# A new order of the pieces, and new engines for 250 of them, from the last weight decodes to the end of a fused attention and cosine feed-forward kernel

## The chip, the core and the metric

The kernel runs on one core of a Trainium2 chip. The metric is the device time of one execution in microseconds (us), and the median of several executions is compared. TensorE (PE) does the matrix products, VectorE (DVE), ScalarE (ACT) and GpSimd (POOL) the work on elements, and SyncE (SP) issues nearly all DMAs.

## What is computed

Attention inside chunks of 64 tokens, then a feed-forward layer whose activation is h·cos(h):

```python
scores = scale * np.matmul(q_c, k_c.transpose(0, 1, 2, 4, 3))
scores = scores - np.max(scores, axis=-1, keepdims=True)
attn = np.exp(scores)
attn = attn / (np.sum(attn, axis=-1, keepdims=True) + 1e-09)
out = np.matmul(attn, v_c)
...
h = x @ w_in
g = h * np.cos(h)
return (g @ w_out).astype(np.float32)
```

There are 8 batches, 8 heads, 576 tokens and 64 columns a head, so x has 4608 rows of 512; w_in is 512x2048 and w_out 2048x512, both given as float64. Every large product is made of three in a rounded format (high by high, high by low, low by high), so each operand has a high part, which is a rounded copy, and a low part, which is the value less its high part.

## The kernel before

Tokens are worked in nine tiles of 512 (t = 0 to 8). Tiles 0 and 1 go through the layer directly, while the 32 weight blocks are decoded from float64 and split. From tile 2 on, block products by a scheme with seven instead of eight products (combinations of weight blocks, kept in device memory and streamed back) take the place of plain ones: `two_pairs` for tile 2, and `block_pair` with `block_products` for the tiles in twos (3 and 4, 5 and 6, 7 and 8, numbered u = 1, 2, 3). The attention of a later tile is woven into the products of an earlier one: `scores_now(t, g)` and `weighted_now(t, g)` for each half g of the heads. Each of these hands PE two pieces, one for each pair of heads, and each piece is 32 small 64x64 products.

All work is put down first as 3646 pieces by `piece(...)` (engine, length, function, the pieces that it waits for). Two tuples then decide everything else: `RANK` gives each piece its place in one list, and `ELSEWHERE` names the pieces that run on their other engine (DVE work on POOL, or ACT copies on DVE). `in_order` (L311) sorts, and a loop at L2527 issues the pieces in that order. Every engine, and SP with its DMAs, therefore executes its own pieces strictly in the order of the ranks, and a piece that waits holds up all that stand behind it on its engine. The ranks are written out by hand into the file; nothing is planned when the program is built.

Names that the steps below use, with what they run on:

- `out_piece` (L1504), `block_piece` (L1831), `prod` in `block_pair` (L1857): products on PE; line L352 in the profile. A `block_piece` of one pair is three 256-column products, `prod` is six of 512 columns.
- `prod` comes in the order A11, S3, S2, A12, S1, A22, S4. S2 waits for `copy_b` on ACT (L1018), which waits for A11; S4 waits for `add_b` on DVE, which waits for S1; with a later tile's attention to weave in, the next A11 waits for `copy_last` on ACT, which waits for S4.
- `parts_of_g` (L1535): the high part on ACT or DVE, then the low part on DVE or POOL (L369 and L367 are the copies, L373 the two-input operations).
- `sum_piece` (L1968), `w_load` (L2059), `wide_x` (L2370): sums of blocks and splits, on DVE or POOL and on ACT or DVE.
- `turned` (L612, operations at L686): six transposes on DVE, ahead of `weighted_now`; its two results are taken out of PSUM by ACT or DVE (L2365), and only then may PE use these banks for the next product.
- `g_load` (L2094): a stored sum is loaded back by SP, split by ACT or DVE and then DVE or POOL, and multiplied on PE.

```python
place = sorted(range(len(work)), key=lambda i: (rank[i], i)) if rank else range(len(work))
return [(i, work[i][8][0] if i in elsewhere else work[i][0]) for i in place]
...
for i, by in in_order(work, RANK, ELSEWHERE):
    work[i][2](*([by] if work[i][8] else []))
```

Of the kernel before, what the change touches and what calls it, by code (L numbers as in the profile page):

```python
# [95 lines left out]
    214, 240, 245, 251, 262, 258, 265, 268, 277, 266, 250, 267, 281, 284, 283, 274, 286, 290, 294, 287, 280, 291,  # L96
    306, 311, 300, 293, 314, 324, 327, 321, 313, 329, 333, 338, 331, 328, 339, 343, 344, 340, 342, 361, 362, 365,
    350, 354, 359, 371, 374, 377, 368, 379, 383, 386, 391, 375, 394, 398, 400, 401, 388, 403, 415, 419, 405, 397,
    408, 410, 418, 431, 427, 435, 439, 441, 434, 417, 438, 440, 443, 446, 444, 454, 458, 461, 452, 455, 467, 469,
    475, 0, 12, 1, 3, 4, 5, 2, 7, 8, 10, 6, 13, 19, 21, 9, 17, 23, 27, 16, 26, 31, 11, 14, 20, 24, 29, 32, 37, 41,  # L100
# [6 lines left out]
    249, 213, 239, 229, 233, 225, 248, 254, 264, 269, 278, 282, 263, 272, 243, 252, 273, 270, 271, 275, 285, 288,  # L107
    298, 302, 279, 255, 259, 276, 261, 296, 299, 304, 307, 317, 319, 301, 289, 295, 292, 297, 308, 527, 303, 305,
    309, 532, 310, 529, 548, 316, 318, 320, 322, 334, 336, 315, 330, 312, 335, 326, 325, 341, 345, 348, 351, 356,
    337, 346, 349, 332, 323, 347, 353, 357, 360, 363, 378, 358, 370, 367, 355, 352, 366, 369, 373, 376, 385, 390,  # L110
    372, 404, 409, 364, 393, 381, 387, 389, 392, 413, 416, 384, 420, 402, 380, 406, 395, 399, 407, 412, 425, 429,
    396, 428, 432, 414, 421, 453, 457, 473, 460, 464, 476, 480, 483, 487, 491, 510, 513, 545, 559, 530, 547, 555,
    556, 557, 562, 565, 572, 577, 575, 597, 576, 579, 587, 594, 598, 604, 614, 620, 636, 640, 411, 433, 430, 426,
    436, 422, 424, 442, 445, 448, 451, 437, 465, 423, 470, 447, 450, 462, 466, 471, 478, 485, 474, 449, 456, 459,
    463, 482, 484, 486, 496, 500, 504, 481, 488, 498, 468, 472, 489, 494, 502, 507, 509, 516, 505, 501, 503, 495,
    492, 512, 515, 517, 518, 523, 526, 514, 546, 511, 519, 560, 520, 528, 531, 542, 564, 567, 525, 544, 549, 535,
    522, 536, 540, 543, 550, 554, 561, 552, 537, 574, 558, 541, 569, 585, 588, 592, 595, 599, 563, 596, 584, 581,
    590, 571, 582, 591, 603, 605, 613, 602, 570, 593, 578, 586, 608, 611, 622, 625, 630, 633, 616, 628, 610, 607,
    612, 634, 638, 621, 623, 617, 629, 619, 626, 627, 631, 635, 637, 641, 642, 632, 660, 624, 643, 654, 645, 652,
    656, 667, 673, 675, 647, 676, 657, 646, 674, 659, 661, 664, 678, 691, 696, 679, 687, 665, 670, 662, 686, 689,  # L120
    697, 701, 706, 713, 704, 700, 692, 698, 720, 712, 715, 716, 719, 730, 735, 711, 737, 731, 734, 723, 721, 729,
    733, 739, 744, 748, 725, 382, 497, 534, 553, 589, 490, 658, 521, 477, 479, 493, 499, 538, 506, 508, 524, 533,
    580, 539, 551, 566, 568, 600, 573, 583, 601, 606, 609, 615, 618, 639, 644, 668, 648, 651, 672, 684, 690, 693,
    702, 650, 714, 741, 699, 709, 717, 749, 649, 655, 671, 680, 688, 722, 694, 742, 677, 732, 666, 683, 682, 710,
    669, 681, 653, 663, 724, 728, 718, 726, 736, 738, 727, 753, 756, 767, 773, 800, 802, 791, 794, 822, 824, 813,
    818, 830, 872, 885, 928, 910, 902, 916, 931, 943, 980, 992, 1007, 1031, 1008, 1020, 1075, 1049, 1072, 1079,
    1091, 1087, 1095, 1103, 1114, 1122, 1120, 1152, 1159, 1197, 1179, 1201, 1215, 1211, 752, 740, 842, 755, 766,
    759, 743, 826, 762, 785, 809, 777, 787, 880, 821, 889, 893, 817, 864, 895, 685, 695, 708, 746, 757, 764, 705,
    707, 745, 751, 775, 788, 781, 793, 796, 808, 868, 871, 878, 747, 750, 754, 758, 761, 772, 760, 763, 765, 770,
    779, 814, 806, 886, 891, 894, 904, 927, 938, 703, 768, 769, 771, 778, 776, 774, 780, 784, 783, 782, 786, 803,  # L130
    790, 789, 792, 798, 795, 799, 804, 807, 805, 812, 811, 816, 797, 801, 810, 827, 832, 836, 841, 844, 815, 820,
    825, 829, 819, 823, 828, 833, 835, 838, 862, 845, 847, 858, 851, 853, 940, 876, 896, 874, 861, 865, 921, 945,
    899, 905, 870, 883, 930, 988, 948, 890, 866, 898, 831, 834, 839, 857, 907, 909, 854, 877, 879, 884, 914, 929,
    936, 962, 964, 968, 971, 976, 979, 837, 840, 843, 846, 849, 860, 848, 852, 855, 863, 901, 961, 944, 983, 999,
    1003, 1013, 1033, 1038, 850, 856, 859, 873, 867, 869, 875, 903, 881, 882, 888, 900, 887, 892, 906, 908, 911,
    915, 913, 919, 923, 918, 922, 924, 926, 934, 897, 912, 917, 925, 952, 957, 969, 974, 920, 950, 954, 967, 932,
    935, 939, 946, 949, 953, 1036, 990, 986, 993, 981, 1024, 1040, 1048, 1055, 1074, 985, 989, 1000, 1078, 1025,
    996, 991, 1006, 1012, 1016, 1086, 1043, 933, 937, 941, 942, 951, 955, 958, 960, 959, 987, 956, 963, 977, 966,
    965, 970, 973, 998, 972, 975, 984, 995, 978, 982, 1022, 1002, 1005, 1026, 1009, 1014, 1017, 1011, 1021, 1019,
    1023, 1052, 994, 997, 1004, 1010, 1037, 1047, 1051, 1062, 1015, 1018, 1029, 1050, 1027, 1030, 1034, 1041, 1054,  # L140
    1068, 1076, 1112, 1090, 1110, 1085, 1089, 1099, 1153, 1127, 1146, 1092, 1101, 1148, 1115, 1133, 1131, 1100,
    1116, 1160, 1156, 1150, 1164, 1028, 1032, 1042, 1044, 1046, 1053, 1056, 1057, 1058, 1060, 1065, 1064, 1063,
    1067, 1071, 1073, 1070, 1080, 1083, 1082, 1081, 1094, 1118, 1097, 1102, 1161, 1105, 1108, 1163, 1107, 1111,
    1119, 1123, 1128, 1098, 1104, 1109, 1113, 1125, 1132, 1135, 1140, 1121, 1126, 1138, 1147, 1129, 1142, 1145,
    1151, 1117, 1130, 1136, 1154, 1143, 1139, 1155, 1158, 1220, 1172, 1225, 1249, 1261, 1169, 1245, 1252, 1157,
    1162, 1236, 1229, 1178, 1176, 1167, 1168, 1231, 1250, 1181, 1244, 1248, 1234, 1256, 1258, 1059, 1066, 1061,
    1084, 947, 1039, 1069, 1077, 1141, 1174, 1173, 1185, 1088, 1134, 1144, 1149, 1182, 1192, 1170, 1093, 1177, 1186,
    1001, 1045, 1096, 1137, 1180, 1184, 1124, 1165, 1190, 1195, 1175, 1189, 1106, 1199, 1035, 1191, 1166, 1171,
# [2434 lines left out]
```

## Time and profile before

| what | us |
|---|---|
| median of 3 executions | 771.12 |
| lowest and highest of them | 770.82, 772.03 |
| the profiled execution | 769.23 |
| its span, first to last instruction | 767.4 |
| PE busy in the span | 753.0 |
| DVE, ACT, POOL busy | 678.1, 530.0, 345.0 |

The page of the profile gives shares of the whole span. The timeline gives instructions in order of time with the idle time of their engine before them; the windows give busy time by stretch. A busy PE is not always a PE at its full rate, since the ends of products are modelled: what counts is the distance from one start to the next, 216 ns for a product of 512 columns here.

### The profile page before, as it was taken

The numbers are of one execution on the slowest core, as the hardware profiler recorded it, in microseconds if no ns is written. First come the engines' busy times: TensorE is split into PE (matmuls) and PEld (weight loads), VectorE is DVE, ScalarE is ACT, GpSimd is POOL, SyncE is SP. The second block draws the span as 40 slices with busy tenths as digits, with TensorE's granted clock in tenths as the row PEclk, the third lists the DMA queues.
The fourth block names the chain that finished last, engine by engine and source line by source line (L and its number), as shares of the span: only waits on it lengthen the run. The fifth ranks groups of instructions, "written<-read, shape, count | busy, mean of one in ns | idle before, by whom it ended". The sixth has DMA issues, their size and how long they took to land.

```text
span 767.4 us, 18052 instructions
## 1 busy us (share of the span) xinstructions
PE 753.0 (98%) x6676; PEld 681.3 (89%) x6676; DVE 678.1 (88%) x1138; ACT 530.0 (69%) x1066; POOL 345.0 (45%) x329
## 2 busy tenths in 40 slices
PE   7999999999999999999999999999999999999998
PEld 6888888888999888888889997888899989989997
DVE  6998889888999998989999979989999889878975
ACT  6999786466875557878786659779786566567532
POOL 3421244635599316746622246547501136464233
PEclk9999999999999999999999999999999999999999
DMA  9994332199988948888899946899899567999982
GB/s 340 410 420 156 131 125 95 58 308 361 343 298 298 315 152 294 293 307 259 310 345 378 368 166 227 284 307 325 286 383 341 170 199 250 306 314 335 362 286 91
DMA packets 127000, 210.92 MB, mean 275 GB/s; under 512 B 11712, under 2 KB 67008, under 8 KB 126912
## 3 DMA queue, kind: packets, MB, share of 16 engines
q1 hardware_dynamic: 126336, 208.71, 78.4%
q8 instruction: 53, 0.87, 0.4%
q10 hardware_dynamic: 576, 1.05, 0.4%
q14 instruction: 35, 0.29, 0.1%
HBM read 148.90 MB, written 60.82 MB: 273 GB/s over the span
## 4 chain that ended last, share of the span: by engine, by line
PE 73%; DVE 8%; DMA 7%; ACT 5%; issue 3%; POOL 2%; SPq 1%; ACTq 0%; POOLq 0%; DVEq 0%
PE acc L352 31%; PE h L352 26%; PE a L352 16%; DMA sums<-w_in 4%; DVE w_in L373 2%; DVE w_in L1027 1%; ACT w_in L1024 1%; POOL w_in L373 1%; DMA sums<-g 1%; ACT w_in L1031 1%; SPq L349 1%; DVE w_in L686 1%; DVE w_in L1021 1%; DMA w_in<-diffs 1%; DMA kt<-in_kT_dram 1%
## 5 line engine op out<-in xcount | busy, mean ns | idle before, releaser
L352 PE MATMUL h<-x,w_in 128*128 128x512 f32 (+1 forms) x960 | 224.8, 365 | 0.4 <-DVE w_in L373 0.2
L352 PEld LDWEIGHTS h<-x,w_in 128*128 128x128 f32 x960 | 169.0, 190 | 22.1 <-DVE w_in L373 0.7
L352 PE MATMUL acc<-w_out,g_hi 128*128 128x512 f32 (+1 forms) x720 | 172.7, 330 | 0.0
L352 PEld LDWEIGHTS acc<-w_out,g_hi 128*128 128x128 f32 x720 | 123.8, 190 | 12.4
L352 PE MATMUL acc<-w_out,g_lo 128*128 128x512 f32 (+1 forms) x360 | 117.4, 326 | 0.0
L352 PE MATMUL h<-w_in,w_in 128*128 128x512 f32 (+1 forms) x384 | 98.6, 355 | 1.2 <-ACT h L1018 1.1
L373 POOL TENSOR_TENSOR w_in<-w_in,w_in 128x512 f32<-128x512 f32 (+2 forms) x41 | 48.9, 1197 | 60.2 <-ACT w_in L1031 24.5
L352 PEld LDWEIGHTS h<-w_in,w_in 128*128 128x128 f32 x384 | 65.4, 190 | 10.9 <-ACT h L1018 2.9
L352 PEld LDWEIGHTS acc<-w_out,g_lo 128*128 128x128 f32 x360 | 68.6, 190 | 4.7
L369 ACT CAST g_hi<-w_in 128x512 fp32r<-128x512 f32 x71 | 44.0, 623 | 33.4 <-PE acc L352 9.2
L1031 ACT ACTIVATE w_in<-w_in 128x512 f32<-128x512 f32 x96 | 57.7, 627 | 12.1 <-DVE w_in L1027 11.8
L373 POOL TENSOR_TENSOR g_lo<-w_in,g_hi 128x512 fp32r<-128x512 f32 x32 | 42.1, 1315 | 36.5 <-ACT g_hi L369 17.9
L373 DVE TENSOR_TENSOR g_lo<-w_in,g_hi 128x512 fp32r<-128x512 f32 x62 | 45.5, 738 | 4.2 <-ACT g_hi L369 3.5
L369 ACT CAST g_hi<-x 128x512 fp32r<-128x512 f32 x52 | 32.2, 624 | 21.8 <-PE acc L352 12.3
L1024 ACT ACTIVATE w_in<-w_in 128x512 int32<-128x512 f32 x56 | 34.2, 627 | 16.8 <-DVE w_in L1021 11.9
L373 POOL TENSOR_TENSOR g_lo<-x,g_hi 128x512 fp32r<-128x512 f32 x9 | 12.2, 1362 | 74.2 <-ACT g_hi L369 74.2
L373 POOL TENSOR_TENSOR g_lo<-g,g_hi 128x512 fp32r<-128x512 f32 x18 | 23.6, 1314 | 45.9 <-ACT g_hi L369 19.9
L352 PE MATMUL a<-w_in,w_in 128*128 128x512 f32 (+1 forms) x204 | 43.1, 350 | 1.0 <-ACT w_in L369 0.7
L352 PE MATMUL a<-x,w_in 128*128 128x512 f32 (+1 forms) x192 | 41.2, 353 | 0.0
L352 PE MATMUL acc<-w_in,g_hi 128*128 128x256 f32 x240 | 41.0, 275 | 0.0
L1027 DVE SCALAR_TENSOR_TENSOR w_in<-w_in,w_in 128x512 f32<-128x512 int32 x56 | 37.8, 698 | 3.4 <-ACT w_in L1024 2.8
L373 DVE TENSOR_TENSOR g_lo<-x,g_hi 128x512 fp32r<-128x512 f32 x47 | 36.5, 789 | 4.5 <-ACT g_hi L369 4.2
(317 smaller groups left out, 1953.0 us busy)
## 6 DMA issues: line engine op xcount, KB each, us to landing
w_in<-combo SPq DMA_DIRECT2D x84, 512.0 KB, 5.5
w_in<-sums SPq DMA_DIRECT2D x64, 256.0 KB, 5.0
combo<-w_in SPq DMA_DIRECT2D x56, 256.0 KB, 3.8
w_in<-combo SPq DMA_DIRECT2D x56, 256.0 KB, 5.4
x<-sums SPq DMA_DIRECT2D x48, 256.0 KB, 5.0
qt<-in_qT_dram SPq DMA_DIRECT2D x36, 256.0 KB, 5.2
w_in<-in_w_in_dram SPq DMA_DIRECT2D x16, 512.0 KB, 9.3
kt<-in_kT_dram SPq DMA_DIRECT2D x32, 256.0 KB, 5.3
```

What stands on the lines that cost most here:

```text
L349: kept(nc.sync.dma_start(out=out, in_=in_))
L352: kept(nc.tensor.matmul(*args, **kw))
L369: kept(nc.scalar.copy(out=out, in_=in_))
L373: kept(eng.tensor_tensor(out, a, b, op=op))
L686: kept(nc.vector.transpose(out=dst[o : o + BL, :, qb], in_=src[i : i + BL, :, 1 - qb]))
L1021: kept(nc.vector.tensor_tensor(out, a, b, op=ALU.add))
L1024: kept(nc.scalar.activation(g.bitcast(I32), h, AF.Identity, bias=0.25, scale=0.5 / math.pi))
L1027: kept(nc.vector.scalar_tensor_tensor(g, g.bitcast(I32), -2.0 * math.pi, h, op0=ALU.mult, op1=ALU.add))
L1031: kept(nc.scalar.activation(g, g, AF.Sin, bias=0.5 * math.pi))
```

## The change

Only the numbers in `RANK` and `ELSEWHERE` change. The pieces, their functions and what each waits for stay as they are. The ranks agree up to place 271 of 3646, about 55 us into the profiled execution; of the 962 PE pieces the first 77 keep their places.

```diff
-    214, 240, 245, 251, 262, 258, 265, 268, 277, 266, 250, 267, 281, 284, 283, 274, 286, 290, 294, 287, 280, 291,
-    306, 311, 300, 293, 314, 324, 327, 321, 313, 329, 333, 338, 331, 328, 339, 343, 344, 340, 342, 361, 362, 365,
+    214, 240, 245, 251, 262, 258, 265, 268, 276, 266, 250, 267, 280, 283, 282, 273, 285, 289, 293, 286, 279, 290,
+    304, 310, 299, 292, 314, 325, 328, 322, 312, 330, 335, 340, 332, 329, 342, 347, 349, 343, 346, 367, 370, 373,
...
 ELSEWHERE = (
     4, 8, 9, 13, 18, 19, 23, 24, 29, 33, 34, 38, 39, 48, 53, 54, 58, 59, 63, 69, 78, 83, 98, 103, 108, 113, 114,
-    119, 123, 124, 128, 129, 134, 138, 143, 154, 158, 182, 184, 186, 188, 211, 270, 271, 287, 299, 321, 331, 355,
+    119, 123, 129, 133, 134, 138, 139, 154, 159, 182, 184, 186, 188, 211, 270, 271, 287, 299, 321, 331, 355, 365,
...
```

Read out of the two pairs of tuples, by sorting the pieces by their ranks, one engine at a time:

| attention pieces on PE | places on PE before | places after |
|---|---|---|
| scores, tile 3, g 0 | 172, 175 | 170, 171 |
| weighted, tile 3, g 0 and g 1 | 243, 244; 248, 249 | 246 to 249 |
| weighted, tile 4, g 0 and g 1 | 273, 274; 278, 280 | 275 to 278 |
| weighted, tile 5, g 0 | 367, 373 | 371, 372 |
| scores, tile 6, g 0 | 396, 398 | 398, 399 |
| weighted, tile 6, g 0 | 435, 437 | 435, 436 |
| weighted, tile 7, g 1 | 601, 603 | 605, 606 |

Runs of attention pieces on PE with no other product in them: 38 before, 30 after.

| engine changes | to | count |
|---|---|---|
| ACT copies | DVE | 59 |
| DVE copies | ACT | 41 |
| DVE two-input pieces | POOL | 75 |
| POOL two-input pieces | DVE | 75 |

Pieces on DVE: 1084 before, 1102 after; on ACT 837 and 819; on POOL 275 and 275; on SP 488 and 488. Of the net 18 copies that DVE takes over, 16 copy 512 columns inside SBUF and 2 take a result out of PSUM. Between the 163rd PE piece (172.8 us in the profiled execution) and the 446th (388.2 us) stand 304 DVE pieces before and 317 after.

## Rows read from the trace of the kernel before

**Rows 1.** Page: busy us (share of the span) by engine; the chain that ended last
```profile
PE 753.0 (98%) x6676; PEld 681.3 (89%) x6676; DVE 678.1 (88%) x1138; ACT 530.0 (69%) x1066; POOL 345.0 (45%) x329
PE 73%; DVE 8%; DMA 7%; ACT 5%; issue 3%; POOL 2%; SPq 1%; ACTq 0%; POOLq 0%; DVEq 0%
```
**Rows 2.** Timeline, PE, around attention runs: start, length, operands, count, idle before
```profile
210.78 0.38 PE L352 MATMUL acc<-w_out,g_lo 128*128 128x512 f32 x1
...
213.18 0.70 PE L352 MATMUL acc<-w_out,g_hi 128*128 128x512 f32 x2
...
250.16 0.60 PE L352 MATMUL acc<-w_out,g_hi 128*128 128x512 f32 x2
250.60 0.38 PE L352 MATMUL acc<-w_out,g_lo 128*128 128x512 f32 x1
...
252.00 0.92 PE L352 MATMUL acc<-w_out,w_in 128*128 128x512 f32 x3
...
253.83 0.38 PE L352 MATMUL acc<-w_out,g_lo 128*128 128x512 f32 x1
...
254.76 0.70 PE L352 MATMUL acc<-w_out,g_hi 128*128 128x512 f32 x2
```
**Rows 3.** Windows: us, busy time (instructions) by engine, PE clock, DMA share, GB/s
```profile
172.00:380.00 208.00, 207.67 (x2048) 184.10 (x2047) 190.64 (x317) 148.55 (x350) 124.96 (x126) 1.00 0.87 295
222.00:276.00 54.00, 54.00 (x586) 49.25 (x586) 50.04 (x79) 32.93 (x63) 34.83 (x35) 1.00 0.87 294
350.00:400.00 50.00, 48.15 (x464) 42.61 (x457) 47.47 (x82) 42.67 (x97) 27.93 (x28) 1.00 0.89 303
763.80:767.40 3.60, 0.00 (x0) 0.00 (x0) 0.42 (x1) 0.00 (x0) 0.00 (x0) 0.81 0.34 114
```
**Rows 4.** Timeline, PE, at its longest stops behind 300 us
```profile
381.64 1.56 PE L352 MATMUL a<-w_in,w_in 128*128 128x512 f32 x6 [0.70 <-ACT w_in L369]
395.06 0.49 PE L352 MATMUL a<-w_in,g_hi 128*128 128x256 f32 x2 [0.74 <-ACT g_hi L369]
395.86 0.38 PE L352 MATMUL a<-w_in,g_lo 128*128 128x256 f32 x1 [0.31 <-DVE g_lo L373]
466.08 0.48 PE L352 MATMUL h<-w_in,w_in 128*128 128x512 f32 x1 [0.27 <-ACT h L1018]
558.34 0.49 PE L352 MATMUL a<-w_in,g_hi 128*128 128x256 f32 x2 [1.35 <-ACT w_in L369]
627.45 0.48 PE L352 MATMUL h<-w_in,w_in 128*128 128x512 f32 x1 [0.34 <-ACT h L1018]
```
**Rows 5.** Timeline, PE, at a small stop ahead of the product S4
```profile
372.88 1.46 PE L352 MATMUL a<-x,w_in 128*128 128x512 f32 x6
374.43 0.92 PE L352 MATMUL h<-w_in,w_in 128*128 128x512 f32 x3
```
**Rows 6.** Timeline, SP and ACT, ahead of the stop at 558 us
```profile
551.10 2.74 SPq L349 DMA_DIRECT2D x<-sums  x4
557.20 0.61 ACT L369 CAST g_hi<-x 128x512 fp32r<-128x512 f32 x1
```
**Rows 7.** Groups by line: busy us, mean ns of one; then two rows of DVE's timeline
```profile
L369 ACT CAST g_hi<-w_in 128x512 fp32r<-128x512 f32 x71 | 44.0, 623 | 33.4 <-PE acc L352 9.2
L367 DVE CAST w_in<-w 128x512 fp32r<-128x512 f32 x11 | 4.6, 419 | 0.1
L373 POOL TENSOR_TENSOR g_lo<-w_in,g_hi 128x512 fp32r<-128x512 f32 x32 | 42.1, 1315 | 36.5 <-ACT g_hi L369 17.9
L373 DVE TENSOR_TENSOR g_lo<-w_in,g_hi 128x512 fp32r<-128x512 f32 x62 | 45.5, 738 | 4.2 <-ACT g_hi L369 3.5
753.77 1.53 DVE L373 TENSOR_TENSOR g_lo<-w_in,g_hi 128x512 fp32r<-128x512 f32 x1
758.01 1.28 DVE L373 TENSOR_TENSOR x<-g,x 128x512 fp32r<-128x512 f32 x2
```
**Rows 8.** Timeline, ACT, ahead of the stop at 381.64 us
```profile
381.00 0.59 ACT L369 COPY w_in<-a 128x512 f32<-128x512 f32 x1 [0.66 <-DVE w_in L686]
```

399 rows, old and new, of tables (ELSEWHERE, RANK) are left out of this document.

## The prediction

> **What bounds the kernel now.** I read the page first: PE is busy for 753.0 of 767.4 us, and the chain that ended last is PE for 73% [rows 1]. DVE is next with 678.1 us. So the order of the work can win only what PE loses between its products. The windows come second: of the 14.4 us in which PE is idle by the page, 3.6 lie behind the last product [rows 3], and some more in the opening, which the change leaves alone. Third, the timeline of PE alone, since a busy PE hides two kinds of loss. One is the change between 128x128 products and the 64x64 products of attention, which never shows as idle time [rows 2]. The other is the stops: the six in [rows 4] are the longest behind 300 us, 3.7 us of idle time together. Each costs some 0.26 us more than it shows, because a product's modelled tail (380 ns long where the pitch is 216, so 0.16) covers the first part of the wait, and the second product after a stop starts about 0.1 late (from 466.08 to the next start 0.32 instead of 0.22). So the six come to 5.3 us. Ten smaller ones between 156 and 625 us, of 0.13 to 0.54 us from start to start beyond the pitch (one of them in [rows 5]), add some 4. About 9.5 us of stops lie in the part that changes. The clock is granted in full throughout [rows 3], so no time is to be had there.
>
> **The joins of attention pieces.** The change makes 30 runs of attention pieces on PE out of 38. The price is read from starts. A piece alone: the last product ahead starts at 253.83, is due to make way at 254.05 (216 ns), and the next large one starts at 254.76; its pair lasts 0.70 where an undisturbed one lasts 0.60 [rows 2]. That is 0.71 + 0.10 = 0.81 us. Two together: 250.60 + 0.22 = 250.82 to 252.00, and 0.10 again, 1.28 us. Four together: 210.78 + 0.22 = 211.00 to 213.18, and 0.10, 2.28 us [rows 2]. Six split pairs are joined (scores of tiles 3 and 6, weighted of tiles 4, 5, 6 and 7): 6 × (2 × 0.81 − 1.28) = 2.04 us. Two pairs of pairs become one run (weighted of tiles 3 and 4): 2 × (2 × 1.28 − 2.28) = 0.56 us. Together 2.6 us, on PE itself, which sets the end: nothing has to hide it. The joins can give back part of this only by waiting, which comes below.
>
> **Stops that get shorter.** At 558.34 the first product of the last stage of tiles 5 and 6 waits for a loaded sum: SP issues four loads from 551.10 on, and ACT makes the high part from 557.20 to 557.81 [rows 6]. The issue waits for the product A22 of the pair before. Between that product and the first one that waits stand 13 PE pieces before and 15 after, the added ones being of 0.34 us (three products of 256 columns, 112 ns each): 0.67 us off a stop that shows 1.35 [rows 4]. The like stop of tiles 3 and 4, at 395.06 and 395.86, keeps its 0.74 + 0.31: the same PE work stands ahead of it. At 308 and 374 us the product S4 waits for `add_b`, 0.25 us beyond the pitch at the second (372.88 + 6 × 0.216 to 374.43, [rows 5]) and 0.14 at the first, read likewise; one and five more pieces of 0.34 us stand in between after the change, so both should go, 0.4 us with 0.1 each for the restart, 0.6 in all. The stops at 466.08 and 627.45 (S2 behind `copy_b` [rows 4]) have the same PE work ahead of them in both orders: they stay. Sum: 1.3 us gained.
>
> **Places that get tighter.** In four places (tiles 5, 6, 7 and 8) the next A11 waits for `copy_last`, and the PE work between S4 and A11 shrinks, in three of them from six pieces or five to a weighted pair alone (about 1.1 us against a product's tail and a copy of 0.59, as in [rows 8]). That fits if ACT is free at that moment, and costs up to 0.6 if it finishes something else first: 0 to 0.6 each. The second half of tile 4's joined run needs a bank that a chain of four operations (two on ACT, two on DVE, 0.6 to 0.74 each by [rows 7, 8], 2.7 to 2.9 us) must release; PE work ahead of it is about 2.9 us: 0 to 0.45. One `out_piece` of tile 0 moves six PE places forward, close behind its low part: 0 to 0.4. Ends: 0 to 3.2 us. These are ordinary small waits like the many that cost nothing in this trace, so I take a value near the lower end, 0.7.
>
> **The engines that change.** POOL takes 1315 ns for a low part that DVE makes in 738, ACT 623 ns for a copy that DVE makes in 419 [rows 7]. The 75 pieces that go either way between DVE and POOL nearly cancel (on DVE some 2 us more). The net 18 copies cost DVE more: two operations in a row last 1.28 where one alone lasts 0.68, so a long operation costs the queue 0.60 and a copy 0.42 − 0.08 = 0.34 [rows 7]. That is 16 × 0.34 + 2 × 0.60 = 6.6 us, with the first part about 9 us on top of 678. ACT and POOL lose work, and neither bounds anything (69% and 45%). The 9 us do not lie evenly: between 172.8 and 388.2 us of this trace DVE has 13 more pieces between the same PE pieces, nine long ones, two copies and two groups of four short sums (4 × 0.34): 5.4 + 0.7 + 2.7, about 9. From 172 to 380 us DVE is busy 190.64 of 208 us, while PE stops for 0.33 [rows 3]. So 17.4 us idle there become about 7, and with the time that the joins save fewer. What that costs the trace does not show directly. Lower end: nothing, as from 222 to 276 us, where DVE is busy 50.04 of 54 and PE never stops [rows 3]. Upper end: the stretch from 350 to 400 us, where DVE is busy 47.47 of 50 (95%) and PE is idle 1.85 [rows 3]; of that 0.70 is the stop at 381.64, behind DVE's transposes and a copy of their product [rows 4, 8], and 1.05 the loaded sum [rows 4]. With what a stop costs beyond its idle time, 0.70 is about 1.0, and four such stretches give 4 us. I take 0.8, nearer to the lower end, because DVE would still have some 3% to spare there, and because what PE waits for next can stand ahead of the less urgent work in the queue: the ranks order both.
>
> The Trainium skill's page "VectorE: DVE Perf Modes", section "The DRAIN you can't avoid", says that a Vector operation starts only when the pipe of the one before is empty, and exempts what it calls not held. By the full wait two operations would last 1.36 us, not 1.28, and the added DVE work would be some 11 us, not 9. The trace shows the overlap, so the exempt case holds here.
>
> SP's order moves too (394 of its 488 pieces change place), and a DMA that waits holds up those behind it. No PE stop in the changed part is put down to a DMA by itself except through the two loaded sums above. The loads of tile 2's queries, which are moved past one or two stores of partial results, are wanted only some 45 us later. I cost that at nothing; without this cover it would be one load's time, under 6.1 us from issue to first use by [rows 6], once. The end stays as it is: the last store waits for the last DVE addition, and two other stores stand ahead of it in both orders.
>
> **Sum.** Against the profiled execution: 769.23 − 2.6 − 1.3 + 0.7 + 0.8 = 766.8. That execution is 1.9 us below the median of 771.12, so as a median I forecast 768.7.
>
> **Rivals.** First, the gain is given back: the tight places and DVE together cost 3 us or more, so 2.6 + 1.3 is used up and the time is 769.6 to 772.6, say 771. For it speaks that DVE loses over half of its spare time where most of the joins are; against it that the joins themselves cost no other engine anything. Second, DVE becomes the bound between 172 and 388 us: a queue that is never empty delays every chain from PSUM and back. It decides once contention or an order less lucky for the urgent pieces takes the remaining 7 us of slack: the low parts on DVE last 738 ns in the mean, and a single one 1.53 us [rows 7]. At four stretches of 1.85 lost, 7.4 instead of 0.8, the time is 768.7 + 6.6, about 775: slower. Third, the other stops move as well: the stops that I left in place (some 8 us) depend on which piece ACT or DVE holds at that instant, and a third of them may go, 766.
>
> **How the numbers follow.** Forecast 0.50, between 766.9 and 769.6; the third rival 0.08; the first 0.27; the second 0.15. Some 0.2%, 1.5 us, is what a measurement of this kernel can tell from no change: faster is below 769.6, slower above 772.7. Faster 0.57, same 0.27, slower 0.16. For the range, the lower end is 771.1 − 3.9 with 1.6 of the third rival, 765.6. The upper takes in DVE's upper end and two thirds of that of the tight places, which hardly all wait at once: 771.1 − 3.9 + 4 + 2.1 = 773.3. It leaves out most of the second rival and a little of the third.
>
> **What would show it.** Right: 30 runs of 64x64 products, each pair about 1.28 us; the stop of the last stage of tiles 5 and 6 down to about 0.7; PE busy near 749 with a span near 765; DVE busy near 685. Wrong: PE idle time between 172 and 388 us over 2 us with DVE busy above 95% there (second rival); new stops at the A11 after `copy_last`, with ACT as the releaser (first rival).

## The result

| kernel | median, us | ratio to the kernel before, 95% interval |
|---|---|---|
| before, six executions beside the changed one | 771.25 | |
| changed | 775.23 (773.30 to 778.09) | 1.0053 (1.0031 to 1.0074) |
| changed, timed once more on another chip (e13) | 776.15 | 1.0064 (1.0044 to 1.0084) |

The change makes the kernel slower by about 4.5 us: 4.1 and 4.9 by the two ratios, 4.0 and 5.4 by the medians. I had forecast 768.7, between 765.6 and 773.3. The profiled execution of the changed kernel took 775.80 with a span of 774.0, against 769.23 and 767.4 before.

### The profile page after: what moved, and what is told of

Same layout as the page of the kernel before. It is cut to its first block, busy times and chain, and to the rows that moved or that the text cites. A ratio compares the mean times of both kernels' runs of the same rounds, so it can differ in the third digit from the quotient of the medians.

```text
span 774.0 us, 18012 instructions
## 1 busy us (share of the span) xinstructions
PE 755.3 (98%) x6676; PEld 682.7 (88%) x6676; DVE 684.3 (88%) x1157; ACT 522.6 (68%) x1048; POOL 338.9 (44%) x328
## 4 chain that ended last, share of the span: by engine, by line
PE 70%; DVE 12%; DMA 6%; ACT 4%; issue 3%; POOL 2%; SPq 1%; ACTq 0%; POOLq 0%; DVEq 0%
PE acc L353 28%; PE h L353 27%; PE a L353 15%; DVE w_in L374 2%; DMA sums<-w_in 2%; DVE w_in L1028 2%; DMA kt<-in_kT_dram 1%; DVE g_lo L374 1%; SPq L350 1%; ACT w_in L1025 1%; POOL g_lo L374 1%; DMA w_in<-sums 1%; DMA w_in<-combo 1%; DVE w_in L1022 1%; DMA qt<-in_v_dram 1%
## 5 line engine op out<-in xcount | busy, mean ns | idle before, releaser
L353 PE MATMUL h<-x,w_in 128*128 128x512 f32 (+1 forms) x960 | 225.4, 365 | 0.2
L353 PEld LDWEIGHTS h<-x,w_in 128*128 128x128 f32 x960 | 169.9, 190 | 22.2 <-ACT a L1019 0.7
L353 PE MATMUL acc<-w_out,g_hi 128*128 128x512 f32 (+1 forms) x720 | 171.8, 329 | 0.1
L353 PEld LDWEIGHTS acc<-w_out,g_hi 128*128 128x128 f32 x720 | 124.1, 190 | 12.3 <-ACT g_hi L370 0.5
L353 PE MATMUL acc<-w_out,g_lo 128*128 128x512 f32 (+1 forms) x360 | 117.8, 327 | 1.4 <-DVE g_lo L374 1.4
L353 PE MATMUL h<-w_in,w_in 128*128 128x512 f32 (+1 forms) x384 | 99.0, 356 | 1.8 <-ACT h L1019 1.1
L353 PEld LDWEIGHTS h<-w_in,w_in 128*128 128x128 f32 x384 | 64.9, 190 | 12.0 <-ACT h L1019 2.4
L353 PEld LDWEIGHTS acc<-w_out,g_lo 128*128 128x128 f32 x360 | 68.6, 191 | 7.1 <-DVE g_lo L374 2.4
L374 POOL TENSOR_TENSOR w_in<-w_in,w_in 128x512 f32<-128x512 f32 (+2 forms) x37 | 45.1, 1227 | 51.6 <-ACT w_in L1032 17.9
L374 POOL TENSOR_TENSOR g_lo<-g,g_hi 128x512 fp32r<-128x512 f32 x18 | 26.5, 1471 | 65.6 <-DVE g_hi L368 27.3
L353 PE MATMUL a<-w_in,w_in 128*128 128x512 f32 (+1 forms) x204 | 43.2, 351 | 1.4 <-ACT w_in L370 0.5
L353 PE MATMUL a<-x,w_in 128*128 128x512 f32 (+1 forms) x192 | 41.3, 353 | 0.0
L353 PE MATMUL acc<-w_in,g_hi 128*128 128x256 f32 x240 | 41.3, 275 | 0.0
L353 PE MATMUL acc<-x,g_hi 128*128 128x256 f32 x232 | 39.7, 275 | 0.0
```

Of the source, the lines that this page charges most:

```text
L353: kept(nc.tensor.matmul(*args, **kw))
L374: kept(eng.tensor_tensor(out, a, b, op=op))
```

## The profile after

The page of the changed kernel: busy us by engine, and the chain that ended last. The lines of the code are one higher than before (L353 for L352, and so on).

```profile
PE 755.3 (98%) x6676; PEld 682.7 (88%) x6676; DVE 684.3 (88%) x1157; ACT 522.6 (68%) x1048; POOL 338.9 (44%) x328
PE 70%; DVE 12%; DMA 6%; ACT 4%; issue 3%; POOL 2%; SPq 1%; ACTq 0%; POOLq 0%; DVEq 0%
```

Beside [rows 1], DVE has 6.2 us more work, ACT 7.4 less. PE does the same 6676 instructions, of which the joins save some 2.7 us, and yet is busy 2.3 us longer: part of its work ran at a lower speed, or stops hide behind the modelled tails of the products ahead of them. Both are found below. DVE's share of the chain went from 8% to 12%.

The windows (us, then busy time and instructions of PE, weight loads, DVE, ACT and POOL, granted clock, DMA share, GB/s) answer to [rows 3]:

```profile
172.00:380.00 208.00, 206.16 (x2046) 183.30 (x2045) 196.89 (x335) 145.23 (x343) 115.47 (x117) 1.00 0.87 290
222.00:276.00 54.00, 52.91 (x587) 48.79 (x586) 52.03 (x84) 30.96 (x65) 29.07 (x30) 1.00 0.89 301
380.00:430.00 50.00, 46.97 (x414) 44.86 (x413) 42.33 (x72) 33.13 (x61) 11.28 (x11) 0.97 0.92 301
398.00:400.00 2.00, 2.00 (x12) 2.00 (x11) 2.00 (x4) 1.53 (x3) 0.00 (x0) 0.50 0.94 280
```

From 172 to 380 us PE is idle for 1.84 us where it was 0.33, with DVE busy for 94.7% of the time. In the last row PE's clock is granted at 0.50, which is 1.2 GHz, its lower level.

The timeline of PE at its larger stops (start, length, operands, count, idle time before and who ended it), beside [rows 4]:

```profile
224.18 0.48 PE L353 MATMUL acc<-w_out,g_lo 128*128 128x512 f32 x1 [0.29 <-DVE g_lo L374]
235.71 0.27 PE L353 MATMUL h<-e,w_in 64*64 64x64 f32 x2 [0.71 <-PE a L353]
...
396.51 0.46 PE L353 MATMUL a<-w_in,g_hi 128*128 128x256 f32 x2 [2.18 <-DVE g_hi L368]
397.22 0.58 PE L353 MATMUL a<-w_in,g_lo 128*128 128x256 f32 x1 [0.24 <-DVE g_lo L374]
...
558.05 0.38 PE L353 MATMUL acc<-w_out,g_lo 128*128 128x256 f32 x1 [1.11 <-DVE g_lo L374]
...
632.13 0.48 PE L353 MATMUL h<-w_in,w_in 128*128 128x512 f32 x1 [0.86 <-ACT h L1019]
...
729.16 0.38 PE L353 MATMUL acc<-w_in,g_lo 128*128 128x256 f32 x1 [1.20 <-POOL g_lo L374]
```

What a reader can do with two orders of the same pieces is to take products that have nearly the same pieces ahead of them in both, and compare the time from one to the next. I took four, named by their time before: the product A11 that starts at 299 us, the A22 at 387 us, an S4 at 460 us, and a block piece of the last stage of tiles 5 and 6 at 560 us. Times from starts in the traces, us, the first from a product at 73 us:

| kernel | 73 to 299 | to 387 | to 460 | to 560 | to the last product |
|---|---|---|---|---|---|
| before | 225.40 | 88.19 | 73.03 | 99.85 | 203.70 |
| changed | 227.19 | 86.66 | 77.67 | 100.32 | 204.91 |
| changed again (e13) | 227.35 | 87.17 | 75.82 | 99.16 | 204.76 |
| six joins alone (e3) | 224.68 | 86.89 | 73.83 | 98.80 | 203.87 |
| changed, twelve DMAs put back (e10) | 227.66 | 86.99 | 74.67 | 100.08 | 204.23 |
| changed with three mends (e11) | 227.23 | 86.88 | 76.20 | 99.57 | 203.00 |

In the new order the first column holds 0.65 us more product work and the second 0.65 less, since one piece stands ahead of that A11 that stood behind it; in the same way the fourth holds 0.67 more and the fifth 0.67 less. With this taken out, the first profile of the changed kernel loses 1.1 us by the first of these products, wins 0.9 back by 387 us, loses 4.6 around 396 us, and 1.9 behind 560 us. The joins should have gained 2.3 us by 387 us: that gain is gone by then.

## The experiments

Twelve kernels were run first, and three more for what was then open. All medians are in us; "before" is the kernel before on the same chip in the same hours.

| run | median | before | ratio, 95% interval |
|---|---|---|---|
| e1 new order, old engines | 795.83 | 770.92 | 1.0323 (1.0293 to 1.0352) |
| e2 old order, new engines | 794.34 | 770.92 | 1.0300 (1.0275 to 1.0325) |
| e3 six joins alone | 768.77 | 770.92 | 0.9978 (0.9959 to 0.9996) |
| e4 new up to 388 us | 774.11 | 770.92 | 1.0042 (1.0026 to 1.0058) |
| e5 changed, three loads later | 777.79 | 772.00 | 1.0073 (1.0044 to 1.0101) |
| e6 new from 388 to 560 us | 773.96 | 772.00 | 1.0016 (1.0003 to 1.0029) |
| e7 new from 560 us, one execution | 772.30 | 772.00 | |
| e8 joins, five loads later | 773.50 | 772.00 | 1.0019 (1.0001 to 1.0038) |
| e9 SP's order near 380 us alone | 774.98 | 770.88 | 1.0050 (1.0032 to 1.0067) |
| e10 changed, SP's old order there | 774.67 | 770.88 | 1.0042 (1.0028 to 1.0056) |
| e11 changed with three mends | 774.64 | 770.88 | 1.0048 (1.0027 to 1.0069) |
| e12 new up to 300 us | 773.07 | 772.18 | 1.0016 (0.9999 to 1.0033) |
| e13 changed again | 776.15 | 770.74 | 1.0064 (1.0044 to 1.0084) |
| e14 joins, new from 560 us | 770.25 | 770.74 | 0.9989 (0.9975 to 1.0003) |
| e15 six joins again | 768.74 | 770.74 | 0.9964 (0.9947 to 0.9981) |

### e1 and e2: order and engines apart

```diff
 e1                        e2
-RANK = old                 RANK = old
+RANK = new                -ELSEWHERE = old
 ELSEWHERE = old           +ELSEWHERE = new
```

e1: 

> The new order with the old choice of engines. Theory A, the 250 changes of engine made it slower (urgent copies queue behind other work on DVE, a low part lands on POOL): with the old engines the six joined pairs show, so 768 to 770 us, 0.997 of the kernel before, and the stop near 396 us is no longer than the 0.9 us of before. Theory B, the order made it slower (pieces stand closer behind what they wait for): 774 to 776, 1.004 to 1.006, with stops near 224, 235, 396 and 558 us as in the changed kernel. Theory C, only both together do it, since each was found for the other: between 771 and 774 for this one, with stops in new places.

e2: 

> The old order with the new choice of engines. Theory A (the engines made it slower): 774 to 777 us, 1.004 to 1.008, PE stops of 2 us and more behind low parts on POOL or copies on DVE. Theory B (the order made it slower): within 1 us of 771.3. Theory C (order and engines were found together, and half of the change is worse than the whole): slower than 776, with more than 18.4 us of PE stops, which is what the changed kernel has behind 55 us.

Either half costs 3%, five to six times as much as both together. Theories A and B fall; C holds, and more than it said, since I had put e1 between 771 and 774. The waits of PE in e1 and in e2 (who was waited for, us in total, times, longest), the first rows of each:

```profile
PE h L341 <- DMA w_in<-combo: 3.1, 3, 1.7
PE h L341 <- DVE g L766: 3.0, 5, 1.6
PE acc L341 <- DVE g_lo L362: 2.8, 3, 1.9
PE h L341 <- DVE w_in L1010: 2.7, 4, 1.5
```

```profile
PE acc L342 <- DVE g_lo L363: 3.4, 7, 0.9
PE h L342 <- ACT h L1008: 2.7, 6, 0.7
PE h L342 <- DVE g L767: 2.5, 3, 1.1
PE a L342 <- DVE g_lo L363: 2.2, 3, 1.2
```

No place stands out; the stops behind 55 us add up to 39.9 us in e1 and 36.1 in e2, against 9.4 before and 18.4 after. By these two runs an order written out for one set of lengths is wrong all along as soon as 250 pieces have other lengths. Nothing can be read from these two about the blame of either half. The rest of the runs therefore cut the change by time, not by kind.

### e3 and e15: the joins alone

The kernel before, with the second piece of six split attention pairs moved up to the first. For tile 5:

```diff
 PE:
  weighted_now(5, 0), go
+ weighted_now(5, 0), go_on
  block_piece (five of them)
- weighted_now(5, 0), go_on
```

e3: 

> The kernel before, with nothing changed but that in six places the second piece of an attention pair stands right behind the first on PE (scores of tiles 3 and 6, weighted of tiles 4, 5, 6 and 7). If the price of a run of 64x64 products is as read from the trace (0.82 alone, 1.29 for a pair), PE's work falls by 6 x 0.35 = 2.1 us, with 28 runs behind 55 us where there were 34, and the time is 769.2 us, 0.9973. If the pieces that now come 0.5 us later make others wait, or stops elsewhere take up the gain (the rival that it is given back), 771 +- 0.7.

e15: 

> The kernel before with the six joins, once more, to stand beside e14 on one chip: 0.9978 of the kernel before, 768.8 us. Over 0.9990 would mean that the first measurement was luck.

768.77 and 768.74, 2.15 and 2.00 us less than before. The page of e3:

```profile
PE 750.8 (98%) x6676; PEld 680.9 (89%) x6676; DVE 675.8 (88%) x1138; ACT 529.4 (69%) x1066; POOL 344.6 (45%) x329
```

PE's busy time falls by 2.2 us, the 28 runs behind 55 us are 27 pairs and one four, at 1.29 and 2.30, and no other stretch grows by more than the spread of the profiles. This is the version that beats both kernels.

### e4, e6, e7 and e12: the change cut by time

Each takes the new order and engines in one stretch and the old ones elsewhere.

```diff
 pieces sorted by    e12          e4           e6             e7
-                    old          old          old            old
+                    new to 300   new to 388   new 388..560   new from 560
```

e12: 

> The new order and engines up to the first product of a pair of tiles 5 and 6's predecessor stage at 300 us (the 343rd PE piece), the old ones behind, among them SP's old order near 380 us. In five profiles of kernels with the new front PE reaches this product 227.2 to 227.7 us after its 71st piece, in the kernel before after 225.4, of which 0.65 is one more product piece ahead of it: so 1.15 us lost although four joins gain 1.26. Theory G (the waits that the joins and moves cost in this part, near 145, 202, 225, 236 and 255 us, are there on every run): 771 + 1.1 = 772.1 us, 1.0007 to 1.0022, and the same stops of 0.3 to 0.9 us in its profile. Theory H (they are luck of single runs): 769.6 to 771, or less.

e4: 

> The new order and engines up to the product A22 of the first pair of tiles 5 and 6 (the 446th PE piece, 388 us in both profiles), the old ones behind it. In the two profiles this product starts at 388.4 us in both: the gain of the joins and the added stops cancel by then. If that is so on every execution: 771 +- 0.7 us. If the state in which the first part leaves the queues (DMAs still on their way) is what makes the stop near 396 us longer: 773 to 775, and that stop is over 1.5 us though everything behind 388 us is as in the kernel before.

e6: 

> Old order and engines up to the product A22 of the first pair of tiles 5 and 6 (388 us), the new ones from there to the first product of the last stage of tiles 5 and 6, the old ones behind it. The earlier loads are issued as in the kernel before, the copy of the high part is on DVE as in the changed one. Theory D (queue of DMAs): the stop near 396 us is 0.9 to 1.7 us, as in the two profiles with the old issue order, and the time 771 to 773. Theory E (copy on DVE): the stop is over 2 us, and the time 774 or more.

e7: 

> Old order and engines up to 560 us, the new ones behind. In the changed kernel's profile one low part on POOL (moved there from DVE) lasted 3.36 us near 726 us, and PE stopped 1.37 us behind it. If that is what POOL always does there: the same stop again, and a time some 1.4 us above the kernel before beside it. If it was a single event: a POOL operation of 1.3 to 1.7 us, no stop over 0.3 us behind 640 us, and a time within 1 us of the kernel before.

The pieces of the cut add up to the whole: 3.2 us by e4's ratio, 1.2 by e6's and 0.3 by the one execution of e7, each uncertain by 1 us or more. e12 costs 1.2 us by its ratio, as theory G said, with an interval that just touches no change; its profile has the stops of the changed one near 145, 203, 225 and 236 us again. e4 costs 3.2, and its stop near 399 us is 2.8 us of idle time although everything behind 388 us is old: what the first part leaves under way makes it. In e6 this place has the new copy on DVE and the old DMAs ahead, and the stop is short:

```profile
376.71 2.83 PE L341 MATMUL h<-w_in,w_in 128*128 128x512 f32 x6 [2.23 <-DVE w_in L1010]
...
398.38 0.46 PE L341 MATMUL a<-w_in,g_hi 128*128 128x256 f32 x2 [0.31 <-DVE g_hi L356]
```

So theory E, the copy on DVE, falls, and D stands for this stop; the time, 773.96, is above the 771 to 773 that went with D. e6 still costs 1.2 us. The first of its two rows lies in a stretch with the old order, where the kernel before has 0.25 us [rows 5], and the granted clock behind it is 0.50 from 378 to 380 us: single stops of this kind came and went between profiles of one order, all between 310 and 377 us. e7 is one execution, 0.3 us above the median of before; its profile settles POOL, which comes with e11.

### e9: twelve DMAs in another order

The kernel before; SP's queue from 380 to 388 us in the new order, all other queues as before. Z are stores of sums, w and x loads of weight sums, numbered by block:

```diff
-x22 Z22 Z3 x21 w00 w03 w23 Z22' w01 w10 Z3' Z1'
+Z22 Z3 x22 Z1' w00 w03 x21 w10 Z22' w01 Z3' w23
```

> The kernel before; only twelve DMAs that SP issues between 380 and 388 us stand in the order of the changed kernel (the slow load, tile x from diffs, seventh and not fourth, one weight load last and not seventh). All other queues are as before. Theory D (the stop near 396 us hangs on the order of SP's DMAs ahead of the loads of the product sums): these loads land 1 to 2 us later, the stop is over 2 us where two profiles with the old order have 0.9 and 1.4, PE's clock may fall to 1.2 GHz behind it, and the time is 772.5 to 775. Theory F (the order on SP is indifferent, the stop of the changed kernel comes from what ACT and DVE do): stop of 0.9 to 1.7 us and a time within 1 us of the kernel before.

774.98, 4.1 us slower: theory D, at its upper end. The same twelve transfers, none added, cost as much as the whole change. The way from them to PE is seen best in ACT's timeline, where an operation waits until a store from its buffer has landed (the store Z22'). Before, then the changed kernel, then e9:

```profile
389.65 1.15 ACT L1024 ACTIVATE w_in<-w_in 128x512 int32<-128x512 f32 x2 [0.48 <-DMA sums<-w_in]
```

```profile
392.20 0.63 ACT L1025 ACTIVATE w_in<-w_in 128x512 int32<-128x512 f32 x1 [2.39 <-DMA sums<-w_in]
```

```profile
393.30 1.15 ACT L1013 ACTIVATE w_in<-w_in 128x512 int32<-128x512 f32 x2 [2.91 <-DMA sums<-w_in]
```

ACT stands idle for 0.48, 2.39 and 2.91 us, DVE behind it, and the copies of the loaded product sums come only after the work that waited. In e4 the row reads 2.69, in the joins alone 0.46. By the trace's landing times the transfers of SP land one behind the other, 0.65 us apiece for 256 KB, but the load x21 lands 2.67 us behind the one ahead before, 2.23 in the changed kernel, 3.67 in e3 and 2.55 in e4: it is slow in each. In e13 it lands 1.48 us behind. In the old order it is issued at 382.2, in the new one at 383.6 with two more loads ahead of it. Those are slow there too: in the profiles of the changed kernel, e4 and e9 the loads x22, w00 and w03 land 1.0 to 2.4 us apart, where w00 and w03 take 0.65 to 0.70 in the kernel before. So everything behind them, the store and the four loads of product sums, lands later: the second of these loads 6.7 us after the start of A22, against 8.4 in the changed kernel and 8.7 in e9. In e9's timeline and windows:

```profile
398.70 0.78 PE L341 MATMUL a<-w_in,g_hi 128*128 128x256 f32 x2 [3.52 <-ACT g_hi L358]
```

```profile
399.00:401.00 2.00, 1.96 (x9) 1.67 (x9) 2.00 (x5) 1.73 (x4) 0.00 (x0) 0.50 1.02 373
```

The stop is longer than the wait for the store, and PE's clock is at its lower level behind it.

### e5 and e8: loads moved out of the way

e5 is the changed kernel with three weight loads moved behind the four loads of product sums; e8 is the joins with two such moves in tiles 3 and 4, and three in tiles 5 and 6.

```diff
 e5, SP:
-w03 x21 w10 Z22' w01 Z3' w23 sums sums sums sums
+x21 Z22' w01 Z3' sums sums sums sums w03 w10 w23
```

e5: 

> The changed kernel, with one thing moved: three loads of stored weight sums (SP, tile w_in, first used 10 us and more later) are issued behind the four loads of the stored product sums on which the stop near 396 us hangs, not ahead of them. Theory D (the stop is a queue of DMAs: those loads land one behind the other, 0.65 us each, and in the changed kernel the slow one among the earlier ones stands later in the queue): the loads land 3 x 0.65 = 2 us sooner, the stop falls from 2.3 us to about 1, PE's clock stays at 2.4 GHz behind it, and the time is 772 to 773.5. Theory E (the stop is DVE's, which makes the high part behind other work, since its copy was moved from ACT to DVE): the stop stays over 1.8 us, and the time 775.2 +- 0.8.

e8: 

> The kernel before with the six joined pairs, and with five loads of stored weight sums (two in tiles 3 and 4, three in tiles 5 and 6, all first used 8 us and more behind their landing or late in their stage) issued behind the loads of the product sums that PE waits for. By theory D the product sums land 1.3 us sooner at the stop near 394 us (1.71 in the profile of the joins alone) and 1.95 us sooner at the stop near 556 us (1.06): both fall under 0.5 us, and the time is 768.8 - 1.2 - 1.0 = 766.6 us, 0.994 to 0.995 of the kernel before. If these stops are not the DMA queue's, or the loads that now come later stop PE themselves: 768.8 +- 0.7, or more.

Both do what was forecast at the place, and lose elsewhere. e5's timeline of PE and of DVE:

```profile
398.55 0.49 PE L342 MATMUL a<-w_in,g_hi 128*128 128x256 f32 x2 [0.17 <-ACT w_in L359]
...
407.97 0.58 PE L342 MATMUL acc<-w_out,g_lo 128*128 128x256 f32 x1 [2.97 <-DVE g_lo L363]
```

```profile
406.01 0.42 DVE L363 TENSOR_TENSOR w_in<-w_in 128x256 f32<-128x256 f32 x1 [3.20 <-DMA sums<-w_in]
```

The stop of 2.18 has become 0.17, and one of 2.97 stands 9 us later: DVE waits for another store, which the moved loads now precede. e5's profile is of its second longest execution and also has stops of 1.70 and 1.27 us near 315 and 374 us, ahead of the place, which the edit doesn't touch. In e8 the stop near 394 us shrinks from 1.55 to 0.3 us of idle time, and a new one of 1.65 us appears near 567. In this stretch the DMAs are busy all the time (before: share 1.00 and 349 GB/s from 380 to 430 us): a transfer that is moved up puts another one off.

### e10 and e11: the changed kernel mended

e10 puts the twelve DMAs of e9 back. e11 also gives one low part back to DVE and moves one block piece back.

```diff
 e11 on top of e10
-3458 (a low part of a loaded sum) on POOL
+3458 on DVE
 PE near 558 us:
-2555 2580 2556 2480 2478 weighted 2544 2554 2557 2611
+2580 2556 2480 2478 weighted 2544 2554 2557 2555 2611
```

e10: 

> The changed kernel; only the same twelve DMAs stand in the order of the kernel before. Theory D: the stop near 396 us is about 1 us where the changed kernel has 2.3, the clock stays, no new stop near 408 us (nothing is issued later than in the kernel before), and the time is 772 to 773.5 instead of 775.2. Theory F: stop over 2 us, 775 +- 1.

e11: 

> The changed kernel with three mends: the twelve DMAs in the old order; the low part of one loaded sum, which the change gave to POOL, back on DVE (PE stopped 1.29 to 1.37 us behind it in three profiles); and the one block piece that stopped PE near 558 us put behind the three pieces that follow it there. If these three places hold what the change lost behind 388 us, their stops (2.3 with the clock's 1.6, 1.37, 1.27) go or shrink to the 0.9 of the kernel before, 5 us less at most in the profile: 770 to 772 us, no slower than the kernel before. If the stops only move on to the next piece: over 773.

In the profiles the mends work. e10's stop near 396 us:

```profile
395.60 0.49 PE L342 MATMUL a<-w_in,g_hi 128*128 128x256 f32 x2 [0.18 <-ACT w_in L359]
```

e11 has no stop over 0.3 us behind 540 us save the one of `copy_b` near 630 (0.86 us of idle time with the new tail, in the kernel before 0.34 and another of 0.25 just ahead of it). The spans of the two are 770.9 and 770.2 us where the changed kernel has 774.0. But the medians, 774.67 and 774.64, are 3.8 us above the kernel before beside them, and the changed kernel is 4.0 and 5.4 above: only 0.2 to 1.6 is given back. Both profiles are of the shortest execution of their kernel (772.71 of ten, 771.99 of nine). So, nearly, is that of the kernel before (769.23, where the lowest of 22 is 769.07), and like with like the two are 3.5 and 2.8 us longer than its 767.4. By the table of stretches, with the product work taken out, e10 loses 1.6 us in the first, 1.6 in the third and 1.2 in the last, and wins 0.6 and 0.4 in the others. The clock isn't it: nine of e10's ten executions and all nine of e11's have a granted clock of 0.999 or 1.0, and still most take 774 to 776. Theory D's forecast for the median fails here, and I leave it open why the same twelve DMAs cost 4.1 us on the old kernel and give back so little on the new.

These twelve are also not the whole of SP's new order: in 385 of its 488 places the queue of e10 still differs from that of the kernel before. PE's waits show what the rest does. The first row is from e13's timeline, the second from e11's waits:

```profile
370.57 0.45 PE L353 MATMUL h<-w_in,w_in 128*128 128x512 f32 x1 [0.83 <-DMA w_in<-combo]
```

```profile
PE h L342 <- DMA w_in<-combo: 1.4, 2, 1.1
```

With SP's old order between 300 and 560 us (before, e2, e3, e7, e12, e14, e15) PE waits for no DMA from 100 us on. With the new order there it waits for loads of weight sums (`w_in<-combo`) in every profile: 0.3 and 1.5 us in the two of the changed kernel, 0.6 in e10, 1.4 in e11, 1.9 in e4 and e5, 0.6 in e6, 3.1 in e1. The changed kernel with the whole of SP's old order was not run.

One low part on POOL takes over 3 us in three profiles, of the changed kernel, e5 and e7. POOL's and DVE's timeline in the changed kernel, then in e7:

```profile
725.75 3.36 POOL L374 TENSOR_TENSOR g_lo<-g,g_hi 128x512 fp32r<-128x512 f32 x1 [2.93 <-ACT g_hi L370]
...
727.30 0.68 DVE L374 TENSOR_TENSOR x<-x 128x512 fp32r<-128x512 f32 x1
728.53 1.13 DVE L374 TENSOR_TENSOR g_lo<-w_in,g_hi 128x512 fp32r<-128x512 f32 x1 [0.55 <-ACT g_hi L370]
```

```profile
722.60 3.26 POOL L362 TENSOR_TENSOR g_lo<-g,g_hi 128x512 fp32r<-128x512 f32 x1 [3.04 <-ACT g_hi L358]
...
724.05 0.68 DVE L362 TENSOR_TENSOR x<-x 128x512 fp32r<-128x512 f32 x1
725.37 1.04 DVE L362 TENSOR_TENSOR g_lo<-w_in,g_hi 128x512 fp32r<-128x512 f32 x1 [0.64 <-ACT g_hi L358]
```

The mean of this operation on POOL is 1.3 us [rows 7]. Here DVE runs four operations without a pause beside it, until 727.98 and 724.73, and POOL's ends 1.13 us after that in both cases (729.11 and 725.86), as if it had begun only then. In e10 and e13 the same low part stands beside the same operations, takes 1.71 and 1.86 us, and a copy on DVE beside it takes 1.50 where it takes 0.41 in the others: there DVE seems to be the one that waits. The Trainium skill's page "SBUF — State Buffer", section "SBUF: two separate sides", says that DVE and GpSimd share a pair of ports, which for some operations one of them holds for the whole operation while the other waits; the rows agree with that, on either side.

### e13 and e14: an ordinary execution, and the tail

e13 is the changed kernel, unaltered. e14 is e3 with the new order and engines from 560 us on, the low part 3458 on DVE.

```diff
 e14, from 560 us of before, in the last stage of tiles 5 and 6:
-old order and engines
+new order and engines, 3458 on DVE
```

e13: 

> The changed kernel once more. If the execution profiled first was an ordinary one: a stop of 2.2 us or more near 396 us, with the clock at 1.2 GHz behind it, and a granted clock of 0.998 or less in nearly all executions, as in the kernels e4 and e9. If it was one of the worse ones: a stop of 1 to 2 us without a fall of the clock, 1.000 in most executions, and the loss in the fixed waits and in other stops. Time 775 +- 1 in either case.

e14: 

> The kernel before with the six joins up to the last stage of tiles 5 and 6 (the fourth block piece of it, 560 us), the new order and engines behind, save that the low part which took POOL 3.3 us is on DVE. In the profiles with the new tail and that mend PE needs 203.0 us from this piece to its last product, in those with the old tail 203.7 to 203.9: 0.7 us less than the joins alone, 768.1 us, 0.9965 of the kernel before. If the tail's other stops differ from run to run as those near 396 do: no better than the joins alone, 768.8 +- 0.7.

e13's timeline of PE and of ACT, and its clock:

```profile
396.75 0.46 PE L353 MATMUL a<-w_in,g_hi 128*128 128x256 f32 x2 [1.36 <-DVE g_hi L368]
```

```profile
392.44 0.63 ACT L1025 ACTIVATE w_in<-w_in 128x512 int32<-128x512 f32 x1 [1.57 <-DMA sums<-w_in]
```

```profile
398.00:400.00 2.00, 2.00 (x13) 1.99 (x12) 2.00 (x5) 1.29 (x3) 0.00 (x0) 0.58 1.06 357
```

The stop is there again, shorter, and so are the wait for the store and the fall of the clock. Of the nine executions five have a granted clock of 0.998 or less and four do not, so neither expectation holds whole: the fall comes in five of them at most, since the stretch behind the last product lowers the mean too [rows 3]. The four with the clock above that are no shorter (774.73 to 777.25, against 773.16 to 776.59), so the fall of the clock isn't what sets the median either. In e9 all six lie at 0.998 or less, in e4 eight of eleven. e14 is 1.5 us slower than the joins alone on the same chip: the tail is not worth keeping, and my 0.7 from the sums of two profiles was less than the tails differ from execution to execution.

## Why the prediction was wrong, step by step

**The joins**: right. Behind 55 us there are 23 pairs at 1.29, three runs of four at 2.29 and no piece alone, where there were 12 alone, 21 pairs and one four: 2.7 us without the waits that lie inside, 2.6 forecast. By themselves six of them bring 2.0 to 2.15 us, 2.04 forecast.

**SP's order at nothing**: this is the step of the sum that failed, as far as the runs show it. I wrote that no PE stop is put down to a DMA except through the two loaded sums, and costed the 394 moved DMAs at nothing; and of the stop at 395 us that it keeps its length, since "the same PE work stands ahead of it". The cover was counted in PE's work, and the landing of the loads was taken as fixed. It isn't: twelve DMAs in another order cost 4.1 us on the old kernel (e9). And where the new order of SP stands, PE waits for loads of weight sums, 0.3 to 1.9 us by profile, where it waits for none with the old one. How much of the 4.5 in an ordinary execution this is, is not shown: with the twelve put back (e10) the stop and the fall of the clock are gone, and 3.8 us of the loss stay, with the rest of SP's new order in place. The row that would have warned me is ACT's wait of 0.48 us for a store at 389.65, quoted above from the trace of before, together with a DMA share of 1.00 from 380 to 430 us. I had read the waits of PE alone, and a window (350 to 400 us) in which the share is 0.89 [rows 3].

**Places that get tighter**: mis-sized, the second term that failed. I took 0.7 of 0 to 3.2. The profile has 0.49 near 145, 0.21 at 202, 0.45 at 224, 0.25 at 255 and 0.52 at 329 us, which is near 2 us beyond the kernel before; and 0.86, the largest, was not on my list: the run of four of tile 3, at 235.71, waits in its middle for the bank that the chain of work must release. I had priced that join at a gain of 0.28. All of these up to 255 us return in e10, e11, e12 and e13 at the same sizes. e12 shows this part in its time: 1.2 us slower where its joins should have brought 1.3, so some 2.5 us of waits ahead of 300 us alone. The four A11 behind `copy_last`, for which I had set up to 0.6 each, don't wait in either profile of the changed kernel: the sign of the first rival did not show.

**Stops that get shorter**: half right. The two stops ahead of S4 at 308 and 374 us are gone in both profiles, and a like one, 0.33 us of idle time, is new at 528 us in both. The one at 558 us is gone too, but the first profile has 1.27 us a few pieces ahead of it: one of the "added pieces of 0.34 us" that were to be cover is itself not ready until DVE ends its low part at 558.0. Stops from 545 to 600 us: 1.61 before, 1.65 and 0.74 in the two profiles of the changed kernel, against −0.67 forecast.

**DVE**: too dear in work, and the rival did not come. 6.2 us more between 172 and 380 us, not 9; 11.1 us of slack left there, not 7; PE idle 1.84 and DVE busy 94.7%. I had set the mark of the second rival for 172 to 388 us, over 2 us and above 95%: there the two profiles have 2.35 and 2.98 us, over it, with DVE at 94.6% and 94.2%, just under it (before: 1.03 us). The 11 us that I named for the full wait between operations come to 10 by my own terms (16 × 0.42 + 2 × 0.68 + 2); nothing hangs on it. That rival gave 775, the measured time, but for another reason: A22 starts at 386.92 and 386.95 us in the two profiles, and what the profile lost went behind it. A time that agrees shows no cause.

**POOL and DVE that "nearly cancel"**: wrong for one piece. At the mean of 1.3 us the low part 3458 would have been ready in time; it took 3.4 in the first profile, and PE stopped 1.37 us; in e13 it took 1.86 and PE did not wait for it.

**The range**: the clock was full in [rows 3] save behind the last product, and I took it as given. A longer stop brought it down, which the range had no term for. By e13 and e11 that is a part of the profiled time, and not of the median's distance.

**What stays open.** e4 bounds the loss by place (3.2 us are made by what is ordered before 388 us), and e12 gives 1.2 of them to the part before 300. With the twelve DMAs in the old order the parts come to 2.7 us by ratio (e12 1.2, e6 1.2, e7 0.3), where e10 has 3.2: no loss clear of the noise is left for the pieces between 300 and 388 us. So the 4.5 us have no single cause. Waits ahead of 300 us make some 1.2 net of the joins, and what is ordered from 300 to 388 us, SP's DMAs among it, some 2. How the rest divides between SP's order and that of the other engines, no run here tells.

Summed over the first profile: joins −2.7, other stops and the clock +9.2, of which the stretch from 387 to 460 us holds 4.6; 6.5 in all, and the span grew by 6.6. This is the account of that one execution.

## What to carry to other kernels

When a fixed order changes, follow the stores as well as the loads: an engine that waits for a buffer's store is an engine that waits for everything ahead of it in the DMA queue, and where the DMAs are busy all the time a transfer's landing depends on its place. An order and a choice of engines that were found together can't be judged or kept by halves: each alone cost 3%. A gain that is on the bounding engine itself, such as fewer changes of its mode, can be taken alone, and here that is worth more than the whole change.

## What the runs showed of the hardware

**The clock can fall behind a stop of one to three us.** PE was idle for 2.18 us before 396.51 in the changed kernel and had a granted clock of 0.50 from 398 to 400 us: two products of 256 columns started 0.42 to 0.43 apart where the pitch is 0.22. The 19 products from 397.22 on took 3.84 us until 401.06 instead of 2.13, 1.7 us lost besides the stop. In e13 it fell after 1.36 us of idle time, in e3, after 1.55 us, it did not (1.00 from 392 to 398 us): the length of the stop alone doesn't decide it.

**Loads of one size land unevenly**: the load x21 comes 1.5 to 3.7 us behind the landing ahead of it in seven profiles, most others of its 256 KB 0.65, and w00 and w03 0.65 to 0.70 in the old order but 1.0 to 2.4 in the new one. No run here shows why.

**POOL and DVE can keep each other waiting**: beside an unbroken row of DVE operations a low part on POOL took 3.3 to 3.4 us instead of 1.3 in three profiles; in two others it took 1.7 and 1.9, and a DVE copy beside it 1.50 instead of 0.41.
